# Two fixed experts instead of three, and ScalarE scaling in the low-part route of the expert weights

## The chip, the cores and the metric

One core of a Trainium2 chip runs the whole program. The metric is the device time of one execution in microseconds (us), with the kernel before and the kernel after run on the same chip. TensorE (PE) multiplies matrices, VectorE (DVE), ScalarE (ACT) and GpSimd (POOL) work elementwise, SyncE (SP) issues most DMA transfers.

## The reference

Attention over 4 batches, 12 heads, 448 positions and 64 columns gives 1792 tokens of 768 numbers. A dense two-matrix layer with a leaky ReLU follows. The last layer is a routed one, and it is the part that the change touches:

```python
skip_score = x @ w_skip
do_compute = skip_score > 0
xc = x[do_compute]
logits = xc @ w_gate
e_idx = np.argmax(logits, axis=1)
...
for e in range(E):
    mask = e_idx == e
    h = np.maximum(xc[mask] @ w1[e], 0.0)
    y[mask] = gate_w[mask, None] * (h @ w2[e])
out[do_compute] = xc + y
```

There are E = 8 experts; w1[e] is 768 x 1024 and w2[e] is 1024 x 768. With the inputs of seed 0, 691 tokens are routed, and the reference gives experts 0 to 7 the counts 155, 107, 80, 162, 52, 62, 65 and 8.

## The kernel before

The program has three stages on one timeline: attention, the dense layer in 8 blocks of tokens, and the experts. The experts' stage is a sequence of eight passes, numbered 0 to 7 here. A pass takes the tokens of one expert, in a fixed number of columns (WIDTHS, line 251), because the program is compiled before the counts are known. The first FIXED passes (line 250) belong to the experts of the same number, 176 columns each. The other passes belong to the other experts ranked by their token counts (`ranks`, `ranked`): the largest gets 176 columns, the next 128, 96, 80 and 64. A fixed expert's weights can be fetched at any time; a ranked expert's can be fetched only when the rank is known, with an address read from a register (`load_ids`, line 1718). Tokens beyond a width are treated in a loop behind everything (line 1817), which runs no time when all fit.

A pass e gathers its rows (POOL, line 1460), turns them by transposes (PE, line 1476; ACT line 1480 writes the high half zh, DVE line 1483 the low half zl), multiplies by w1 ("up e", lines 1443 to 1445, into hp; ACT 1498 and DVE 1501 make hh and hl), multiplies by w2 ("down e", the same lines, into yp; ACT 1515), transposes back (PE, line 1524), adds on DVE (line 1530) and scatters (POOL, line 1536). Every product is three float16 products: high by high, high by low, low by high. So every weight matrix is needed as a high and a low float16 part. Up 0, up 1, down 0, up 2, down 1, up 3, down 2, up 4, down 3, up 5, down 4, up 6, down 5, up 7, down 6, down 7 is the order on PE (`uses`, line 1353; LAG = 3).

A matrix comes in pieces, 12 of 128 x 512 for w1 and 8 of 128 x 768 for w2 (`matrix_steps`, from line 1368). SP loads a piece into one of 8 staging buffers (line 1388). The high part is made by ACT (line 1394) or, where the planner finds ACT busy, by DVE with a tensor_scalar (line 1396). The low part is made by DVE in one scalar_tensor_tensor (line 1401), except for every fourth piece (LO_G = 4) of matrices 6 to 15 of the list, where POOL multiplies the staged piece by 16 (line 1404) and then subtracts the high part (line 1408). The finished matrix lies in one of 6 places: two in a pool "we" (list numbers 0, 1, 6, 7, 12, 13), four in a pool "big" (the others), and in each pool a matrix takes over the place of the one that came four (two) tiles ahead of it in that pool. So number 9 of the list waits until PE has finished number 3. GATE = (4, 4) says which piece is the first that waits until POOL has issued the first gathers; all pieces ahead of it are loaded during the dense layer.

The order on every engine is fixed when the program is built: a planner (`Plan`) with a table of costs picks at each moment the step that can begin first. Each engine then works through its queue in that order on the chip. The planner's costs know nothing of one engine slowing another.

Of the kernel before, what the change touches and what calls it, by code (L numbers as in the profile page):

```python
# [14 lines left out]
AF = mybir.ActivationFunctionType  # L15
ALU = mybir.AluOpType
# [9 lines left out]
SC_W = 16.0  # L26
# [5 lines left out]
class Plan:  # L32
# [50 lines left out]
    def op(self, key, opts, after=(), takes=(), uses=(), dma=False):  # L83


        s = Plan.Step()
        s.dma = dma or (isinstance(opts, tuple) and opts[0] == "Y")
        s.key, s.takes, s.uses = key, list(takes), list(takes) + list(uses)
        s.opts = {}
        for e, ns, f, *h in ([opts] if isinstance(opts, tuple) else opts):  # L90
            hold, more = ns if isinstance(ns, tuple) else (ns, 0)
            s.opts[e] = (hold, more, f, h[0] if h else 0)
        s.outs, s.ready, s.done, s.end, s.engine = [], dict.fromkeys(s.opts, 0), False, 0, None
        s.id = self.count
        self.count += 1
        for b in s.uses:
            b.left += 1
        s.left = 0
        for d in after:
            if d is None:  # L100
                continue
            if d.done:
                self.after(s.ready, d)
            else:
                d.outs.append(s)
                s.left += 1
        if s.left == 0:
            self.enter(s)
        return s
# [97 lines left out]
def attention_moe_routed_experts(  # L207
# [18 lines left out]
    V, A, G, T, Y = nc.vector, nc.scalar, nc.gpsimd, nc.tensor, nc.sync  # L226
# [16 lines left out]
    CAP = 128 + cap2  # L243
# [3 lines left out]
    N_X = 4  # L247


    FIXED = 3  # L250
    WIDTHS = [CAP] * FIXED + [CAP, 128, 96, 80, 64]
    NR = NE - FIXED

    const = ctx.enter_context(tc.tile_pool(name="const", bufs=1))
# [10 lines left out]
    sixteen = const.tile([128, 1], F32, name="sixteen")  # L265
# [47 lines left out]
    op, buf = plan.op, plan.buf  # L313
# [40 lines left out]
    def late_constants():  # L354
# [20 lines left out]
        V.memset(mcount, 0.0)  # L375
        for e, width in enumerate(WIDTHS):
            V.memset(widths[:, e:e + 1], float(width))
# [99 lines left out]
    AHEAD1, AHEAD2 = 2500, 8000  # L477
    LAG = 3
    XFER, TAIL2, N_ST3, UP2 = 1150, 3500, 1, 2740
    GATE, LO_G = (4, 4), 4  # L480
    PLACES = ["st2", "st", "st2", "st", "st2", "st", "st2"] + ["st3"] * N_ST3
    K_WIN, K_WOUT, K_ROUTER = 0, 520, 1200
    done_win = {}
# [867 lines left out]


    uses = sorted([(e, x) for e in range(NE) for x in range(2)], key=lambda u: 2 * u[0] + LAG * u[1])
    b_w, n_w, w_ready, gates = {}, [None], {}, [None]

    def matrix_place(i, pool, name):

        u = uses[i]
        b_w[u] = buf(name)
        b_w[u].left += 1  # L1360

        def new():
            got["we", u] = expert_view(pool.tile([128, BIG], F16, tag="big", name="we"), u[1])

        n_w.append(take(40000 + 100 * i, b_w[u], new, after=n_w[-1:]))
        w_ready[u] = []

    def matrix_steps(i, first=0, last=None):

        e, second = u = uses[i]  # L1370
        n_new = n_w[i + 1]
        src_of = (w1, w2)[second]

        def rows(c):
            if e < FIXED:
                return lambda: src_of[e, c * 128:(c + 1) * 128, :]
            return lambda: src_of[ds(got["id", e], 1), c * 128:(c + 1) * 128, :].rearrange("a p f -> (a p) f")

        for x, (src, at, n) in list(enumerate(expert_pieces(second, rows)))[first:last]:
            got["pieces"] = got.get("pieces", -1) + 1  # L1380
            own = PLACES[got["pieces"] % (len(PLACES) if i >= 6 else 7)]
            b_st = buf(own)
            w = {}

            def load(w=w, src=src, n=n, own=own):
                if "st" not in w:
                    w["st"] = (stage if own == "st" else got[own]).tile([128, DM], F32, tag="st", name="ew")[:, 0:n]
                Y.dma_start(out=w["st"], in_=src())

            def hi(eng, w=w, at=at):  # L1390
                def f():
                    o = at(got["we", u], 0)
                    if eng is A:
                        A.activation(o, w["st"], AF.Copy, scale=SC_W)  # L1394
                    else:
                        V.tensor_scalar(o, w["st"], SC_W, None, op0=ALU.mult)
                return f

            def lo(w=w, at=at):
                h, l = (at(got["we", u], a) for a in range(2))  # L1400
                V.scalar_tensor_tensor(l, w["st"], SC_W, h, op0=ALU.mult, op1=ALU.subtract)  # L1401

            def lo_scale(w=w, n=n):
                G.tensor_tensor(w["st"], w["st"], sixteen.to_broadcast([128, n]), op=ALU.mult)

            def lo_rest(w=w, at=at):
                h, l = (at(got["we", u], a) for a in range(2))
                G.tensor_tensor(l, w["st"], h, op=ALU.subtract)

            def gate(w=w, n=n, own=own):  # L1410
                w["st"] = (stage if own == "st" else got[own]).tile([128, DM], F32, tag="st", name="ew")[:, 0:n]
                G.memset(w["st"][:, 0:1], 0.0)

            key = 40000 + 100 * i + x
            small_ = n < DM
            after, takes, w_uses = [n_new], [b_st], []
            if (i, x) == GATE:

                after = gates[0:1] = [op(key, ("G", 100, gate), takes=[b_st], after=[n_new, gates[0]])]
                takes, w_uses = [], [b_st]  # L1420
            elif (i, x) > GATE:
                after = [n_new, gates[0]]
            if e >= FIXED:
                after = after + [n_ids]
            n1 = op(key, ("Y", (450, XFER * n // 768), load), takes=takes, uses=w_uses, after=after)
            n2 = op(
                key - 0.2,
                [("A", 520 if small_ else 733, hi(A)), ("V", 335 if small_ else 469, hi(V), 500)],
                uses=[b_st, b_w[u]], after=[n1],
            )  # L1430
            if x % LO_G == LO_G - 1 and i >= 6:
                n3 = op(key - 0.25, ("G", 1001 if small_ else 1428, lo_scale), uses=[b_st], after=[n2])
                n3 = op(
                    key - 0.3, ("G", 1113 if small_ else 1596, lo_rest), uses=[b_st, b_w[u]], after=[n3]
                )
            else:
                n3 = op(key - 0.3, ("V", 602 if small_ else 869, lo), uses=[b_st, b_w[u]], after=[n2])
            w_ready[u].append(n3)
# [8 lines left out]
    class Pass:  # L1447
# [99 lines left out]
        def fetch(self, e):  # L1547
# [6 lines left out]
                    k0 - 800, ("G", (1040, n), lambda x=x: self.gather(x)), takes=[self.b_rows[x]],  # L1554
                    after=n_kept + [n_slots, n_ranked if e >= FIXED else None], dma=True,
                )
# [197 lines left out]
    with tc.manual_schedule():  # L1754
# [62 lines left out]
        with tc.For_i(0, nw, 1):  # L1817
# [22 lines left out]
            with tc.For_i(0, NE, 1) as e:  # L1840
# [16 lines left out]
                for w, src, at, n in pieces:  # L1857
                    st = stage.tile([128, DM], F32, tag="st", name="ew")[:, 0:n]
# [55 lines left out]
```

## Time and profile before

| what | us |
|---|---|
| median of 3 runs | 994.85 (991.01 to 997.11) |
| the profiled execution | 991.68 |
| its span, first to last instruction | 989.9 |
| PE busy in the span | 819.5 (83%) |
| DVE busy | 694.2 (70%) |
| ACT busy | 572.6 (58%) |
| POOL busy | 362.3 (37%) |

Times in rows are us from the start of the span. Busy shares are means over the three stages, so a stage is read from its own stretch: the experts' products begin at 817.42 and end at 981.87.

### The profile page before, as it was taken

Reading aid. Unit: us, or ns where it says so; the run is one execution under the profiler, and the core shown is the slowest. Engines: PE = TensorE matmul, PEld = TensorE weight load, DVE = VectorE, ACT = ScalarE, POOL = GpSimd, SP = SyncE. Lnnn points to the kernel's source line nnn. Section 1 sums busy time; section 2 is a strip of 40 time slices with the busy share of each in tenths; the row PEclk is TensorE's granted clock in tenths of the full one; section 3 lists DMA queues with packets and bytes.
Section 4 is the critical chain, followed back from the end, with each engine's and each line's share of the span. In section 5 each row is a group of like instructions: output and inputs, shape, how many; then the busy total and the mean of one; then the engine's idle time right before and its main releaser. Section 6 shows DMA issues by size and latency. Waiting matters only on the chain. (4 is left out here: it accounts for less than half of the span.)

```text
span 989.9 us, 22385 instructions
## 1 busy us (share of the span) xinstructions
PE 819.5 (83%) x8325; PEld 597.1 (60%) x8325; DVE 694.2 (70%) x1611; ACT 572.6 (58%) x1298; POOL 362.3 (37%) x567
## 2 busy tenths in 40 slices
PE   2334448985988998999999899999999859999896
PEld 1213226772545565655665577677686628999896
DVE  6978887798658667888888668242323566889982
ACT  5777887788656665556676556121122336666661
POOL 3545574446325134342332001000101131476893
PEclk9955559986989999999999999999999978999999
DMA  6798988989999999779778956110104458877871
GB/s 187 195 192 201 228 205 174 215 211 213 179 218 191 200 196 187 154 157 171 158 146 169 157 126 223 33 32 29 37 1 161 148 165 303 264 246 254 282 259 34
DMA packets 272834, 170.72 MB, mean 172 GB/s; under 512 B 226086, under 2 KB 239526, under 8 KB 272720
## 3 DMA queue, kind: packets, MB, share of 16 engines
q1 hardware_dynamic: 270464, 161.86, 69.0%
q0 software_dynamic: 1536, 5.42, 1.7%
q10 hardware_dynamic: 720, 1.97, 0.7%
q8 instruction: 67, 1.10, 0.5%
q14 instruction: 47, 0.39, 0.1%
HBM read 100.91 MB, written 14.30 MB: 116 GB/s over the span
## 5 line engine op out<-in xcount | busy, mean ns | idle before, releaser
L1028 PE MATMUL hp<-xh,win 128*128 128x256 f16 (+1 forms) x768 | 193.9, 263 | 3.0 <-DVE gf L1047 3.0
L1029 PE MATMUL hp<-xl,win 128*128 128x256 f16 (+1 forms) x768 | 193.3, 262 | 0.0
L1030 PE MATMUL hp<-xh,win 128*128 128x256 f16 (+1 forms) x768 | 193.2, 262 | 0.0
L1116 PE MATMUL zp<-wout,g_h 128*128 128x384 f16 (+1 forms) x448 | 149.6, 334 | 4.6 <-ACT g_h L1054 2.6
L1118 PE MATMUL zp<-wout,g_l 128*128 128x384 f16 (+1 forms) x448 | 149.0, 333 | 0.4 <-DVE g_l L1061 0.4
L1117 PE MATMUL zp<-wout,g_h 128*128 128x384 f16 (+1 forms) x448 | 148.8, 332 | 0.0
L1401 DVE SCALAR_TENSOR_TENSOR we<-ew,we 128x512 f16<-128x512 f32 (+1 forms) x136 | 133.9, 1026 | 13.6 <-ACT we L1394 13.2
L911 DVE SCALAR_TENSOR_TENSOR p<-sp,r,p 128x448 f16<-128x448 f32 x168 | 111.0, 679 | 37.9 <-ACT p L905 37.0
L890 ACT ACTIVATE sp<-sp,m 128x448 f32<-128x448 f32 x168 | 102.0, 609 | 50.1 <-DVE m L884 48.6
L877 PE MATMUL sp<-qkT 64*64 64x448 f16 (+1 forms) x672 | 92.6, 417 | 45.3 <-DVE p L911 21.9
L905 ACT ACTIVATE p<-sp,r 128x448 f16<-128x448 f32 x168 | 103.2, 636 | 44.9 <-DMA pt<-p 19.5
L1394 ACT ACTIVATE we<-ew 128x512 f16<-128x512 f32 (+1 forms) x158 | 106.1, 710 | 25.5 <-DMA ew<-in_moe_w_dram 21.9
L884 DVE TENSOR_REDUCE m<-sp 128x2 f32<-128x896 f32 x96 | 92.7, 968 | 18.8 <-PE sp L877 18.5
L1047 DVE SCALAR_TENSOR_TENSOR gf<-gf,oma,hp 128x256 f32<-128x256 f32 (+1 forms) x128 | 50.5, 441 | 63.6 <-ACT gf L1043 63.5
L1028 PEld LDWEIGHTS <-win 128*128 128x128 f16 x768 | 76.0, 99 | 27.6 <-issue 12.9
L877 PEld LDWEIGHTS <-qkT 64*64 64x64 f16 (+1 forms) x672 | 28.4, 117 | 91.2 <-issue 67.8
L1029 PEld LDWEIGHTS <-win 128*128 128x128 f16 x768 | 76.1, 99 | 9.3
L1030 PEld LDWEIGHTS <-win 128*128 128x128 f16 x768 | 76.1, 99 | 6.9
L1445 PEld LDWEIGHTS <-we 128*128 128x128 f16 x768 | 75.6, 100 | 7.4 <-issue 7.4
L1444 PE MATMUL hp<-zl,we 128*128 128x176 f16 (+4 forms) x384 | 71.6, 228 | 6.8 <-DVE zl L1483 6.7
L1061 POOL TENSOR_TENSOR g_l<-gf,g_h 128x512 f16<-128x512 f32 x24 | 32.7, 1361 | 120.7 <-ACT g_h L1054 114.3
L1443 PEld LDWEIGHTS <-we 128*128 128x128 f16 x768 | 75.6, 100 | 0.7
(225 smaller groups left out, 1860.6 us busy)
## 6 DMA issues: line engine op xcount, KB each, us to landing
ew<-in_moe_w_dram SPq DMA_DIRECT2D x96, 256.0 KB, 4.1
ew<-in_moe_w_dram SPq DMA_DIRECT2D x64, 384.0 KB, 5.4
st<-in_moe_w_out_dram SPq DMA_DIRECT2D x31, 384.0 KB, 4.0
st<-in_moe_w_in_dram SPq DMA_DIRECT2D x28, 384.0 KB, 3.8
qk<-in_k_dram SPq DMA_DIRECT2D x24, 224.0 KB, 3.5
qk<-in_q_dram SPq DMA_DIRECT2D x24, 224.0 KB, 3.3
vf<-in_v_dram SPq DMA_DIRECT2D x24, 224.0 KB, 3.7
zd<-zt SPq DMA_DIRECT2D x14, 384.0 KB, 2.8
```

Of the source, the lines that this page charges most:

```text
L877: T.matmul(out=sp[r, j, 0:S].rearrange("p (j c) -> p j c", j=NJ), lhsT=qT[:, r], rhs=kT[:, :, r], start=(x == 0), stop=(x == last),)
L890: A.activation(e, e, AF.Exp, bias=w["m"][:, x:x + 1], scale=1.0, accum_out=w["s"][:, x, S:S + 1])
L905: A.activation(w["p"][:, x, 0, :], w["s"][:, x, 0:S], AF.Copy, scale=w["r"][:, x:x + 1])
L911: V.scalar_tensor_tensor(p[:, 1, :], w["s"][:, x, 0:S], w["r"][:, x:x + 1], p[:, 0, :], op0=ALU.mult, op1=ALU.subtract)
L1028: T.matmul(out=o, lhsT=win(0, c, m), rhs=xh[:, c, :], start=(c == 0), stop=False)
L1029: T.matmul(out=o, lhsT=win(0, c, m), rhs=xl[:, c, :], start=False, stop=False)
L1030: T.matmul(out=o, lhsT=win(1, c, m), rhs=xh[:, c, :], start=False, stop=(c == KD - 1))
L1116: T.matmul(out=zp, lhsT=gh, rhs=wout(0, kk, ws), start=(kk == 0), stop=False)
L1117: T.matmul(out=zp, lhsT=gh, rhs=wout(1, kk, ws), start=False, stop=False)
L1118: T.matmul(out=zp, lhsT=gl, rhs=wout(0, kk, ws), start=False, stop=(kk == KF - 1))
L1394: A.activation(o, w["st"], AF.Copy, scale=SC_W)
L1401: V.scalar_tensor_tensor(l, w["st"], SC_W, h, op0=ALU.mult, op1=ALU.subtract)
```

## The change

FIXED goes from 3 to 2: passes 0 and 1 keep experts 0 and 1, and six experts are ranked, with widths 176, 128, 96, 80, 64 and 64. A second list `loads` has the matrices of fixed experts first; the weights are fetched, and their places given out, in its order, while PE keeps the order of `uses`. GATE moves to (4, 0), the first piece of matrix 4 of the new list. LO_G goes from 4 to 3, and the multiplication by 16 on the low-part route goes from POOL's tensor_tensor to an ACT activation in place.

```diff
-    FIXED = 3
-    WIDTHS = [CAP] * FIXED + [CAP, 128, 96, 80, 64]
+    FIXED = 2
+    WIDTHS = [CAP] * FIXED + [CAP, 128, 96, 80, 64, 64]
...
-    GATE, LO_G = (4, 4), 4
+    GATE, LO_G = (4, 0), 3
...
     uses = sorted([(e, x) for e in range(NE) for x in range(2)], key=lambda u: 2 * u[0] + LAG * u[1])
+
+    loads = sorted(uses, key=lambda u: u[0] >= FIXED)
...
-        u = uses[i]
+        u = loads[i]
...
-        e, second = u = uses[i]
+        e, second = u = loads[i]
...
-            def lo_scale(w=w, n=n):
-                G.tensor_tensor(w["st"], w["st"], sixteen.to_broadcast([128, n]), op=ALU.mult)
+            def lo_scale(w=w):
+                A.activation(w["st"], w["st"], AF.Copy, scale=SC_W)
...
-                n3 = op(key - 0.25, ("G", 1001 if small_ else 1428, lo_scale), uses=[b_st], after=[n2])
+                n3 = op(key - 0.25, ("A", 620 if small_ else 800, lo_scale), uses=[b_st], after=[n2])
```

The planner sees the new costs and widths, so the queues of the experts' stage come out in another order. Three places of it follow; a number behind a name tells tiles of one name apart.

On DVE, where the low parts of w1 of pass 5 begin; that matrix is tile we_11743 before, and zl_11755 belongs to pass 4, hl_11977 to pass 3:

```order
L1483 SCALAR_TENSOR_TENSOR zl_11755<-zp_11756,zh_11754 128x352
L1483 SCALAR_TENSOR_TENSOR zl_11755<-zp_11834,zh_11754 128x352
L1401 SCALAR_TENSOR_TENSOR we_11743<-ew_11744,we_11743 128x512
L1401 SCALAR_TENSOR_TENSOR we_11743<-ew_11752,we_11743 128x512
L1401 SCALAR_TENSOR_TENSOR we_11743<-ew_11813,we_11743 128x512
L1401 SCALAR_TENSOR_TENSOR we_11743<-ew_11816,we_11743 128x512
L1401 SCALAR_TENSOR_TENSOR we_11743<-ew_11820,we_11743 128x512
L1483 SCALAR_TENSOR_TENSOR zl_11755<-zp_11909,zh_11754 128x352
```

Now (w1 of pass 5 is we_11937, w2 of pass 3 is we_11528, zl_11757 and hl_11942 belong to pass 3):

```order
L1403 SCALAR_TENSOR_TENSOR we_11528<-ew_11697,we_11528 128x768
L1485 SCALAR_TENSOR_TENSOR zl_11757<-zp_11826,zh_11756 128x2x128
L1485 SCALAR_TENSOR_TENSOR zl_11757<-zp_11882,zh_11756 128x2x128
L1532 SCALAR_TENSOR_TENSOR rows_10804<-bp_11989,gate1_155,rows_10804 128x384
L1503 SCALAR_TENSOR_TENSOR hl_11942<-hp2_11943,hh_11941 128x2x128
L1532 SCALAR_TENSOR_TENSOR rows_10804<-bp_12039,gate1_155,rows_10804 128x384
L1503 SCALAR_TENSOR_TENSOR hl_11942<-hp2_11996,hh_11941 128x2x128
L1403 SCALAR_TENSOR_TENSOR we_11937<-ew_11939,we_11937 128x512
L1403 SCALAR_TENSOR_TENSOR we_11937<-ew_11981,we_11937 128x512
```

The matrix used to begin while the turns of the following pass went on, beside down 1; it now begins behind the second hl of up 3.

On POOL, the low parts of w2 of passes 6 (we_12849) and 7 (we_13052) at the end of the stage, before:

```order
L1404 TENSOR_TENSOR ew_13115<-ew_13115,sixteen_75 128x768
L1408 TENSOR_TENSOR we_12849<-ew_13115,we_12849 128x768
L1536 DMA out_0_dram<-rows_11831,sidx1_152 1792x768
L1404 TENSOR_TENSOR ew_13300<-ew_13300,sixteen_75 128x768
L1408 TENSOR_TENSOR we_12849<-ew_13300,we_12849 128x768
L1404 TENSOR_TENSOR ew_13357<-ew_13357,sixteen_75 128x768
L1408 TENSOR_TENSOR we_13052<-ew_13357,we_13052 128x768
```

Now (we_12787 and we_12981):

```order
L1410 TENSOR_TENSOR we_12787<-ew_13488,we_12787 128x768
L1410 TENSOR_TENSOR we_12787<-ew_13560,we_12787 128x768
L1538 DMA out_0_dram<-rows_12231,sidx1_152 1792x768
L1410 TENSOR_TENSOR we_12981<-ew_13664,we_12981 128x768
L1410 TENSOR_TENSOR we_12981<-ew_13766,we_12981 128x768
```

Each pair of POOL instructions has become one; the multiplication by 16 stands in ACT's queue.

On DVE, the last low parts of w2 of pass 7, before (we_13052; zl_13447 belongs to pass 7):

```order
L1401 SCALAR_TENSOR_TENSOR we_13052<-ew_13195,we_13052 128x768
L1401 SCALAR_TENSOR_TENSOR we_13052<-ew_13253,we_13052 128x768
L1483 SCALAR_TENSOR_TENSOR zl_13447<-zp_13508,zh_13446 128x2x64
L1401 SCALAR_TENSOR_TENSOR we_13052<-ew_13397,we_13052 128x768
L1483 SCALAR_TENSOR_TENSOR zl_13447<-zp_13568,zh_13446 128x2x64
```

Now (we_12981; rows_12716 are the rows of pass 6, and their two additions need the whole of down 6):

```order
L1403 SCALAR_TENSOR_TENSOR we_12981<-ew_13615,we_12981 128x768
L1398 TENSOR_SCALAR we_12981<-ew_13716 128x768
L1403 SCALAR_TENSOR_TENSOR we_12981<-ew_13667,we_12981 128x768
L1403 SCALAR_TENSOR_TENSOR we_12981<-ew_13716,we_12981 128x768
L1398 TENSOR_SCALAR we_12981<-ew_13769 128x768
L1403 SCALAR_TENSOR_TENSOR we_12981<-ew_13769,we_12981 128x768
L1532 SCALAR_TENSOR_TENSOR rows_12716<-bp_13941,gate1_155,rows_12716 64x384
L1532 SCALAR_TENSOR_TENSOR rows_12716<-bp_13945,gate1_155,rows_12716 64x384
L1403 SCALAR_TENSOR_TENSOR we_12981<-ew_13775,we_12981 128x768
L1403 SCALAR_TENSOR_TENSOR we_12981<-ew_13779,we_12981 128x768
```

Two high parts of this matrix have come from ACT to DVE, and its last two low parts stand behind the additions of pass 6.

## Rows read from the trace of the kernel before

**Rows 1.** Stretches: length, busy us PE, PEld, DVE, ACT, POOL, then clock, DMA, GB/s.

```profile
880.00:900.00 20.00, 19.95 (x251) 19.38 (x249) 19.79 (x20) 13.33 (x24) 12.92 (x10) 1.00 0.83 263
...
920.00:940.00 20.00, 17.50 (x240) 17.30 (x238) 17.95 (x22) 11.88 (x24) 16.29 (x10) 0.91 0.79 269
...
818.00:975.00 157.00, 149.97 (x2227) 145.32 (x2225) 130.77 (x164) 97.13 (x182) 99.84 (x64) 0.97 0.77 255
903.50:966.90 63.40, 58.53 (x1009) 57.58 (x1007) 57.64 (x70) 40.06 (x79) 54.75 (x34) 0.97 0.77 259
```

**Rows 2.** Groups on PE, 740 to 990: busy, mean ns | idle before, releaser.

```profile
L1444 PE MATMUL hp<-zl,we 128*128 128x96 f16 x48 | 7.8, 225 | 2.5 <-DVE zl L1483 2.5
```

**Rows 3.** Waits of SP's load queue, 740 to 990: total us, times, longest.

```profile
SPq L1388 <- DVE we L1401: 57.9, 47, 9.6
```

**Rows 4.** Groups on DVE, 740 to 990: busy us, mean ns | idle before.

```profile
L1401 DVE SCALAR_TENSOR_TENSOR we<-ew,we 128x768 f16<-128x768 f32 x52 | 60.5, 1196 | 8.0 <-ACT we L1394 7.8
L1401 DVE SCALAR_TENSOR_TENSOR we<-ew,we 128x512 f16<-128x512 f32 x60 | 56.0, 978 | 3.9 <-ACT we L1394 3.8
```

**Rows 5.** DVE in order of time: start, us, instruction.

```profile
805.01 3.55 DVE L1401 SCALAR_TENSOR_TENSOR we<-ew,we 128x768 f16<-128x768 f32 x4
835.09 3.09 DVE L1401 SCALAR_TENSOR_TENSOR we<-ew,we 128x512 f16<-128x512 f32 x5
928.99 3.69 DVE L1396 TENSOR_SCALAR we<-ew 128x512 f16<-128x512 f32 x1
954.43 0.32 DVE L1501 SCALAR_TENSOR_TENSOR hl<-hp,hh 128x160 f16<-128x160 f32 x1
954.66 2.01 DVE L1401 SCALAR_TENSOR_TENSOR we<-ew,we 128x768 f16<-128x768 f32 x1
```

**Rows 6.** POOL in order of time: start, us, instruction.

```profile
929.31 1.66 POOL L1408 TENSOR_TENSOR we<-ew,we 128x768 f16<-128x768 f32 x1
930.91 1.47 POOL L1404 TENSOR_TENSOR ew<-ew,sixteen 128x768 f32<-128x768 f32 x1
955.93 2.24 POOL L1408 TENSOR_TENSOR we<-ew,we 128x768 f16<-128x768 f32 x1
```

**Rows 7.** PE in order of time: start, us, instruction.

```profile
873.07 0.25 PE L1443 MATMUL yp<-hh,we 128*128 128x176 f16 x1
876.72 0.91 PE L1476 MATMUL zp<-ident,rows 128*128 128x128 f32 x4
877.56 0.25 PE L1443 MATMUL yp<-hh,we 128*128 128x176 f16 x1
885.71 0.24 PE L1443 MATMUL hp<-zh,we 128*128 128x176 f16 x1
898.14 0.38 PE L1476 MATMUL zp<-ident,rows 128*128 128x128 f32 x2
898.36 0.24 PE L1443 MATMUL yp<-hh,we 128*128 128x176 f16 x1
915.39 0.50 PE L1524 MATMUL bp<-ident,y 128*128 128x128 f32 x3
917.74 0.49 PE L1524 MATMUL bp<-ident,y 128*48 128x128 f32 x3
977.67 0.19 PE L1443 MATMUL yp<-hh,we 128*128 128x64 f16 x1
981.87 0.49 PE L1524 MATMUL bp<-ident,y 128*64 128x128 f32 x3
```

**Rows 8.** The loads of weight pieces: min, median, max ns, first and last start.

```profile
L1388 SPq DMA_DIRECT2D ew<-in_moe_w_dram x112: 328/333/1523, 818.4 to 964.0; - x112
```

**Rows 9.** Groups of DVE's additions into rows and ACT's high parts, 740 to 990.

```profile
L1530 DVE SCALAR_TENSOR_TENSOR rows<-bp,gate,rows 128x384 f32<-128x384 f32 x10 | 6.1, 612 | 4.3 <-PE bp L1524 4.3
...
L1394 ACT ACTIVATE we<-ew 128x768 f16<-128x768 f32 x64 | 51.9, 837 | 15.6 <-DMA ew<-in_moe_w_dram 12.5 <-PE zp L1118 2.7
```

**Rows 10.** A float32 to float16 copy on DVE elsewhere: min, median, max ns.

```profile
L1056 DVE CAST g_h<-gf x10: 416/426/1391, 184.0 to 704.1; 128x512 f16<-128x512 f32 x10
```

## The prediction, made before the changed kernel ran

> **What bounds the kernel now.** The busy shares of the page mix three stages, so I read the stretch of the experts alone. There PE is busy 149.97 of 157.00 us, DVE 130.77, POOL 99.84, ACT 97.13 [rows 1]. PE looks like the bound, and over most of the stretch it is. But towards the end DVE is full too: 19.79 of 20.00 us from 880 on, 57.64 of 63.40 from 903.5 to 966.9 [rows 1]. The few waits that PE has there end at DVE: up 5 (96 columns) came to a stop for 2.5 us because zl stood behind weight pieces in DVE's queue [rows 2]. The queue of loads waits for DVE as well, 57.9 us in 47 times: a staging buffer comes free when its low part is written [rows 3]. So the experts' stage has two bounds close together: PE's columns, and the rate at which DVE, slowed by POOL, turns pieces into low parts.
>
> That slowing is seen piece by piece. Four pieces of 768 with no subtraction of POOL beside them took 3.55 us, 0.89 each, and five of 512 took 3.09, 0.62 each; a piece of 768 beside POOL's subtraction took 2.01 while that took 2.24 [rows 5, 6]. Over the stage 52 and 60 low parts took 116.5 us [rows 4], where 52 x 0.89 + 60 x 0.62 = 83.5 would do. The 33.0 us of difference fall on 48 POOL instructions (24 pairs): 0.69 us of DVE time for each.
>
> **What the change does, part by part.** *Columns.* One pass of 176 columns becomes one of 64. A group of 48 products of 176 lasts from 873.07 to 876.72, 3.65; 144 of 64 last from 977.67 to 981.87, 4.20 [rows 7]. A pass has 288, so 21.9 becomes 8.4: 13.5 us less. Pass 3 also loses the second half of its transposes: 0.84 per group becomes 0.22, three times [rows 7], 1.9 us. PE has 15.4 us less to do. With seed 0 the ranked counts are 162, 80, 65, 62, 52, 8, which fit 176, 128, 96, 80, 64, 64, so the loop behind stays empty.
>
> *The list of loads.* Number 3 of the list, whose place number 9 takes over, was w1 of pass 2 and is now w2 of pass 1. PE is done with the first at the end of up 2, with the second at the end of down 1. Number 9 is w1 of pass 5 both times. In the order given with the change its first low part now stands behind the second hl of up 3. Up 3 begins at 885.71 - 1.9 = 883.8; two groups of 128 columns with their back transposes take 2 x 2.35 (915.39 to 917.74 [rows 7]); hh and hl add some 0.8. So DVE begins with w1 of pass 5 at about 889.3. Of the pieces behind the gate 52 come first; at the mean rate of before, 145.6 us for 112 loads [rows 8], 1.30 each, they are issued by 886, so nothing earlier is late, and some pieces of pass 5 are staged already. The eight pieces that are no longer loaded ahead of the gate cost nothing for that reason, and the same holds for the gate, which stands behind seven gathers and not eight.
>
> *From there DVE decides*, since seven matrices (68 pieces) are still to be made, while PE, unhindered, needs less time than that. DVE's queue from there to the last low part has, counted in the order: 24 low parts of 768 and 24 of 512, 24 x 0.89 + 24 x 0.62 = 36.3; 14 additions into rows at 0.61 [rows 9], 8.5; 18 hl and 12 zl, which I take like the one of 160 columns at 0.32 [rows 5], 9.6; 16 high parts that the planner gave to DVE (it had 2 in all before, 23 now). A high part is not seen alone in this stage; the nearest row is the copy of 128 x 512, 0.416 at least, 0.426 in the median [rows 10], so 9 x 0.42 + 7 x 0.60 (by the ratio 0.89 to 0.62) = 8.0. That is 62.4. An instruction begins some 0.08 before the end shown of the one ahead (954.43 + 0.32 against 954.66 [rows 5]); for the 60 that are no low parts this takes off 4.8: 57.6. POOL has 20 instructions on the low parts in that time (subtractions alone), at 0.69: 13.8. For the high parts' own waits for POOL I take 0.3 each, 4.8; the ends are 0 (the median copy) and 3.3 (the 3.69 of a high part that began at 928.99 and ended as POOL's 930.91 + 1.47 did [rows 5, 6]), and I lean to the copy because POOL's instructions now stand singly. The sum is 76.2. DVE was busy 99% and 91% in the two rows of its full stretches [rows 1]; at 95% it takes 80.2 us. The last two low parts wait for the additions of pass 6, hence for down 6: 1.5 us more. Down 7 then begins at 889.3 + 80.2 + 1.5 = 971.0, where it began at 977.67 [rows 7].
>
> *ACT* gets 28 multiplications, which I price like its high part of 768, 0.84 us at most [rows 9], 23 us in all, and gives 21 high parts to DVE. Its 97.13 of 157 [rows 1] stay far from full; what could hurt is one such instruction ahead of an hh, 0.84 us, and DVE's backlog hides that. *POOL* loses 24 multiplications (1.47 us for a piece of 768 [rows 6]). That alone ends nothing earlier: its worth is in the 0.69 per instruction, counted above.
>
> **The sum.** Down 7 is 6.7 us earlier, and nothing behind it changes (12.2 us to the end of the span). The profiled execution took 991.68, span 989.9; it would take 985.0. It was 3.2 below the median of the runs shown, so beside that median I say 994.85 - 6.7 = 988.
>
> **The rivals.** *TensorE sets the end.* If DVE keeps up, the 15.4 us of columns come out whole: 994.85 - 15.4 = 979.5, and up to 2.5 less where the wait of up 5 goes too. For it: PE's 149.97 of 157, POOL's shorter route, DVE at 83.5 us for all low parts if POOL left it alone. Against it: the place of w1 of pass 5, which leaves DVE without pieces before 889, and the 16 high parts.
>
> *The high parts on DVE wait for POOL* (slower). Both that DVE had before were hit; if each waits the 3.3 us of the row and not 0.3, the tail grows by 16 x 3.0 / 0.95 = 50 us, to 1038. It decides from small amounts: at 0.40 us more per high part the 6.7 us are gone, at 1.0 us more (16.8 us) the kernel is 1% slower, and at twice that 1022. For it: the row at 928.99, which got in only as two POOL instructions back to back had ended. Against it: ten copies of the same kind with a median of 0.426 and a maximum of 1.391 [rows 10] in stages where POOL works as well. The Trainium skill bears on it: the GPSIMD Engine Reference, section "Key points", says that GpSimd shares its SBUF interfaces with VectorE, in contention with DVE instructions that have two SBUF inputs or run in a 2-port perf mode. The traces agree for the first kind (2.01 against 0.89) and, by the one row, for the second; by that rule the change takes pressure off (28 POOL instructions where there were 48) and puts it on (21 more high parts on DVE).
>
> *The clock.* In the stretch from 920 to 940, with the 2.5 us wait, the granted clock was 0.91 and not 1.00 [rows 1]: some of it ran at the lower of the two levels, 1.2 and not 2.4 GHz. If the longer waits before down 6 and down 7 lead to that for the whole of down 7, its 4.20 us become 8.4: 992. I count this inside the forecast's own range.
>
> *The widths don't fit*, and the loop runs over all eight experts with 160 pieces at 1.30 us: over 200 us more. The counts speak against it.
>
> **How the numbers follow.** The forecast (DVE's tail decides, 988) 0.53, its own range 981 to 996; TensorE's end (979) 0.31; the waiting high parts 0.15; the loop 0.01. About 1%, 10 us, is what a measurement of this kernel tells from no change. Below 984.9 lie the second case and a sixth of the first: 0.40. Above 1004.8 lies most of the third and the loop: 0.13. The rest, 0.47, is within 1%. The range, 973 to 1004, reaches from TensorE's end with its waits gone to the point where the waiting high parts cost 1%.
>
> **What would show it.** Right: DVE without weight pieces shortly before 889 and then full to the end; L1398 (the high parts on DVE) near 0.4 to 0.9 us; some 14 us less slowing on the low parts (28 x 0.69 where there were 33); down 7 near 971, and PE with waits before down 6 and down 7 that end at weights. Wrong: PE without a wait from 817 on (then 979), L1398 with a mean over 1.5 us (then slower), the waits of PE at zl or hh growing because ACT is late, or a first up that no longer begins near 817.

## The result and the profile after

The changed kernel takes 982.55 us (median of 4 runs, 977.27 to 983.59), the kernel before beside it 995.98 (4 runs). The ratio is 0.9865, 95% interval 0.9828 to 0.9901: 13.4 us faster, between 10 and 17. The profiled execution took 983.59, span 981.8; that pair differs by only 8.1 us, since the profile of after reached the last logits 2.2 us later than that of before. Two stretches behind the logits carry the change. From the logits (the start of the last lg on DVE) to the first product of up 0 it is 25.3 us before and 23.1 after. From there to the end of the span, the *stretch* of all that follows, it is 172.5 and 164.4.

Busy time by window after; columns as in [rows 1]:

```profile
818.00:975.00 157.00, 144.42 (x2422) 139.03 (x2419) 128.55 (x190) 104.60 (x202) 69.65 (x42) 0.97 0.79 264
888.00:963.00 75.00, 65.42 (x1349) 63.47 (x1346) 67.77 (x103) 53.89 (x109) 47.43 (x29) 0.97 0.89 294
```

PE has 144.42 us to do where it had 149.97 [rows 1], POOL 69.65 where it had 99.84. From 888 to 963 DVE is the busiest engine. The costliest groups of the weight route, which answer to [rows 4]:

```profile
L1403 DVE SCALAR_TENSOR_TENSOR we<-ew,we 128x768 f16<-128x768 f32 x52 | 56.5, 1107 | 9.1 <-ACT we L1396 8.5 <-POOL we L1410 0.5
L1403 DVE SCALAR_TENSOR_TENSOR we<-ew,we 128x512 f16<-128x512 f32 x56 | 43.4, 807 | 5.4 <-ACT we L1396 5.0
...
L1398 DVE TENSOR_SCALAR we<-ew 128x768 f16<-128x768 f32 x11 | 11.6, 1054 | 1.1 <-DMA ew<-in_moe_w_dram 1.1
...
L1398 DVE TENSOR_SCALAR we<-ew 128x512 f16<-128x512 f32 x12 | 7.3, 615 | 0.0
```

DVE's timeline has the lull and, at the end, the two additions ahead of the last low parts (start, us, instruction, idle time before it and what ended it):

```profile
878.98 0.42 DVE L1485 SCALAR_TENSOR_TENSOR zl<-zp,zh 128x256 f16<-128x256 f32 x1 [0.96 <-ACT zh L1482]
884.41 0.62 DVE L1532 SCALAR_TENSOR_TENSOR rows<-bp,gate,rows 128x384 f32<-128x384 f32 x1 [5.01 <-PE bp L1526]
...
887.63 1.28 DVE L1403 SCALAR_TENSOR_TENSOR we<-ew,we 128x512 f16<-128x512 f32 x2
...
966.35 1.13 DVE L1532 SCALAR_TENSOR_TENSOR rows<-bp,gate,rows 64x384 f32<-64x384 f32 x2 [0.79 <-PE bp L1526]
967.79 2.63 DVE L1403 SCALAR_TENSOR_TENSOR we<-ew,we 128x768 f16<-128x768 f32 x2 [0.31 <-ACT we L1396]
```

And PE's timeline of down 6 and down 7, the rows with a wait ahead of them, which answer to [rows 7]:

```profile
957.49 0.20 PE L1447 MATMUL yp<-hh,we 128*128 128x64 f16 x1 [2.68 <-DVE we L1403]
958.76 0.24 PE L1447 MATMUL yp<-hh,we 128*128 128x64 f16 x1 [0.92 <-DVE we L1403]
...
968.80 0.20 PE L1447 MATMUL yp<-hh,we 128*128 128x64 f16 x1 [1.55 <-POOL we L1410]
969.61 0.20 PE L1447 MATMUL yp<-hh,we 128*128 128x64 f16 x1 [0.55 <-DVE we L1403]
970.48 0.20 PE L1447 MATMUL yp<-hh,we 128*128 128x64 f16 x1 [0.61 <-DVE we L1403]
```

PE now stops in the middle of a matrix, at the product that needs a low part (L1447), for DVE's pieces and for POOL's. After 880 these waits and those for zl sum to 12 us (5.6 and 1.5 in yp, 2.2 and 2.0 in hp, two of 0.4); before, PE waited 5.2 us there, all for zl. Down 7 ends at 974.0 where it ended at 981.87 [rows 7]. Over the whole stretch from up 0 to the end of down 7, before and after (columns as in [rows 1]):

```profile
817.42:982.00 164.58, 157.55 (x2433) 152.68 (x2433) 131.91 (x166) 98.75 (x187) 101.48 (x65) 0.97 0.74 245
```

```profile
817.40:974.20 156.80, 144.26 (x2421) 139.33 (x2421) 128.10 (x189) 104.79 (x202) 69.65 (x42) 0.96 0.79 265
```

PE's busy time fell by 13.3 us, and its idle time rose from 7.0 to 12.5: the columns are most of what was gained, and waits took 5.5 us of it back.

### The profile page after: what moved, and what is told of

It reads as the page before. It is cut to its first block, busy times and chain, and to the rows that moved or that the text cites. A ratio compares the mean times of both kernels' runs of the same rounds, so it can differ in the third digit from the quotient of the medians.

```text
span 981.8 us, 22366 instructions
## 1 busy us (share of the span) xinstructions
PE 806.0 (82%) x8313; PEld 583.5 (59%) x8313; DVE 684.6 (70%) x1626; ACT 576.5 (59%) x1305; POOL 328.2 (33%) x545
## 5 line engine op out<-in xcount | busy, mean ns | idle before, releaser
L1403 DVE SCALAR_TENSOR_TENSOR we<-ew,we 128x512 f16<-128x512 f32 (+1 forms) x132 | 117.3, 919 | 16.3 <-ACT we L1396 15.1
L1396 ACT ACTIVATE we<-ew 128x512 f16<-128x512 f32 (+1 forms) x137 | 93.0, 706 | 24.5 <-DMA ew<-in_moe_w_dram 23.5
L1028 PEld LDWEIGHTS <-win 128*128 128x128 f16 x768 | 75.4, 98 | 28.0 <-issue 13.4
L1447 PEld LDWEIGHTS <-we 128*128 128x128 f16 x768 | 75.7, 100 | 13.0 <-DVE we L1403 6.3
L1445 PEld LDWEIGHTS <-we 128*128 128x128 f16 x768 | 75.7, 100 | 1.3 <-issue 0.5
L1446 PEld LDWEIGHTS <-we 128*128 128x128 f16 x768 | 75.8, 101 | 0.2
L1043 ACT ACTIVATE gf<-hp 128x512 f32<-128x512 f32 x56 | 33.4, 596 | 69.2 <-PE hp L1030 63.6
```

The lines of the kernel that those rows point to most:

```text
L1028: T.matmul(out=o, lhsT=win(0, c, m), rhs=xh[:, c, :], start=(c == 0), stop=False)
```

## The experiments

Twelve kernels in three groups (e1 to e4, e5 to e8, e9 to e12), each group beside runs of the kernel before on the same chip; the last group ran on another chip than the first two. The table puts them side by side; all columns but the last are read from one profile of each kernel. "Start" is when the first high part of number 9 (w1 of pass 5) begins, counted from up 0. "Seven" is the time from there to the last low part of number 15, whoever writes it: the seven matrices 9 to 15, 68 pieces. Both are read by giving the instructions of each engine's timeline, in their order, to the tiles of the program's order (to about half a microsecond).

| kernel | logits to up 0 | stretch | start | seven | ratio to before, 95% |
|---|---|---|---|---|---|
| before | 25.3 | 172.5 | 60.6 | 97.1 | 1 |
| changed | 23.1 | 164.4 | 69.3 | 83.7 | 0.9865 (0.9828 to 0.9901) |
| e1 list and widths, old route | 23.3 | 181.0 | 69.1 | 99.1 | 1.0055 (1.0026 to 1.0083) |
| e2 route alone | 25.0 | 169.1 | 59.8 | 85.0 | 0.9942 (0.9907 to 0.9977) |
| e3 changed, high parts on ACT | 21.3 | 169.1 | 69.4 | 85.8 | 0.9905 (0.9871 to 0.9938) |
| e4 places exchanged, first trial | 31.7 | 154.9 | 61.0 | 82.4 | 0.9892 (0.9852 to 0.9932) |
| e5 changed, no low part on POOL | 23.2 | 157.8 | 69.1 | 76.8 | 0.9850 (0.9809 to 0.9891) |
| e6 changed, 48 columns more | 23.1 | 174.6 | 72.8 | 89.1 | 0.9979 (0.9952 to 1.0007) |
| e7 places exchanged | 28.0 | 151.4 | 57.1 | 81.8 | 0.9826 (0.9787 to 0.9866) |
| e8 as e7, no low part on POOL | 28.5 | 151.0 | 59.2 | 78.2 | 0.9813 (0.9771 to 0.9856) |
| e9 as e7, gate and ids moved | 23.5 | 164.8 | 66.0 | 85.6 | 0.9854 (0.9812 to 0.9896) |
| e10 as e9, no low part on POOL | 23.6 | 150.2 | 59.7 | 78.3 | 0.9727 (0.9689 to 0.9765) |
| e11 before, no low part on POOL | 25.2 | 165.9 | 60.9 | 79.7 | 0.9910 (0.9878 to 0.9943) |
| e12 as e7, old route | 27.9 | 171.1 | 57.6 | 100.7 | 0.9971 (0.9945 to 0.9997) |

Three things are to be seen. *Seven* goes with the route: 97 to 101 us with the old one, 82 to 86 with the new one (89 in e6), 77 to 80 without POOL, whatever the places and the number of fixed experts. *Start* goes by the place of number 9: 57 to 61 where it is the place of w1 of pass 2, 69 where it is that of w2 of pass 1 (66 in e9 and 73 in e6 have causes of their own). And the stretch is start + seven + 11 to 14 us in all but three kernels: in e2 and e11 it is 24 and 25 more (PE's columns for three fixed experts end last there), in the kernel before 14.8, where both come together.

**e1 and e2: each half alone.** e1 is the changed kernel with

```diff
-    GATE, LO_G = (4, 0), 3
+    GATE, LO_G = (4, 0), 4
-                A.activation(w["st"], w["st"], AF.Copy, scale=SC_W)
+                G.tensor_tensor(w["st"], w["st"], sixteen.to_broadcast([128, n]), op=ALU.mult)
```

(and the old cost in the planner); e2 is the kernel before with the new lines.

> The changed kernel with the old route of the low parts: every fourth piece, both instructions on POOL. Two fixed experts, the eight widths and the new list of loads stay. Stretch = from the first product of up 0 to the end of the span (172.5 us in the kernel before, 164.4 in the changed one). Theory A (DVE's weight pieces set the tail, columns and list bring the gain): from the first low part of w1 of pass 5 to the last one DVE has 27 low parts of 512 and 24 of 768 (38.1), 12 additions (7.3), 30 hl and zl (9.6), one high part (0.4), less 3.4 of overlap, plus 34 POOL instructions at 0.69 (23.5): 75.5 / 0.95 = 79.5 us, against 78.7 measured in the changed kernel; stretch 163.5 to 167. Rival B (the route through ScalarE brings the gain): stretch 169 or more, low parts of 768 back at 1.16 us. Theory G (the first gather is slowed by the four low parts that the kernel before has beside it): the first gather takes 1.2 us as in the changed kernel, not 3.4.

> The kernel before with the new route alone: each third piece, its multiplication on ScalarE. Three fixed experts, the old widths and the old list stay. Theory A (TensorE's columns were the bound of the kernel before, and its 5.2 us of waits for zl the only part that DVE held): stretch 168.5 to 171.5, that is 1 to 4 us less than the 172.5 of the kernel before. Rival B (the route brings the gain): stretch 166 or less. Rival C (the 15 high parts on DVE eat what POOL gives back): 172 to 175. Theory G: the first gather is slow again, 3.0 to 3.8 us, since the four low parts of 768 stand beside it; if the list of loads has nothing to do with it, 1.2.

e1 measured 181.0, and is slower than the kernel before: theory A fell, the working of the prediction's tail with it. (The 78.7 us that the expectations of e1 and e5 give for the changed kernel end at the additions of pass 6, 966.35; to the last low part, 970.4, it is 82.8.) e2 measured 169.1, as theory A had it. So 0.55% slower and 0.58% faster make 1.35% faster together. PE's longest waits from 950 on in e1, and POOL's last multiplication and low part:

```profile
957.05 0.20 PE L1445 MATMUL hp<-zh,we 128*128 128x64 f16 x1 [3.10 <-ACT we L1396]
960.25 0.23 PE L1447 MATMUL hp<-zh,we 128*128 128x64 f16 x1 [2.97 <-POOL we L1410]
...
974.03 0.24 PE L1447 MATMUL yp<-hh,we 128*128 128x64 f16 x1 [7.10 <-POOL we L1410]
...
985.15 0.20 PE L1447 MATMUL yp<-hh,we 128*128 128x64 f16 x1 [3.96 <-POOL we L1410]
```

```profile
980.86 1.47 POOL L1406 TENSOR_TENSOR ew<-ew,sixteen 128x768 f32<-128x768 f32 x1 [3.74 <-ACT we L1396]
...
983.45 1.65 POOL L1410 TENSOR_TENSOR we<-ew,we 128x768 f16<-128x768 f32 x1
```

DVE's last low part was written at 970.9, POOL's at 985.1. The low parts on DVE were not slower than before (1168 and 875 ns in the mean, 1196 and 978 in [rows 4]). Over its *seven* DVE was busy 69.83 us of 99.10, so DVE was not what held it:

```profile
886.00:985.10 99.10, 73.83 (x1457) 71.58 (x1454) 69.83 (x98) 56.35 (x113) 71.19 (x45) 0.86 0.68 226
```

It is POOL's queue that came last. The same rows of the kernel before show how near that was:

```profile
971.94 1.47 POOL L1404 TENSOR_TENSOR ew<-ew,sixteen 128x768 f32<-128x768 f32 x1 [0.30 <-ACT we L1394]
973.49 1.64 POOL L1408 TENSOR_TENSOR we<-ew,we 128x768 f16<-128x768 f32 x1
```

The last low part for down 7 is done at 975.1, and down 7 began at 977.67 [rows 7]: 2.5 us to spare, with no PE wait that would have shown it. In the 97 us from 878 on POOL was busy 76.73:

```profile
878.00:975.00 97.00, 91.79 (x1558) 90.23 (x1556) 85.22 (x102) 59.61 (x116) 76.73 (x48) 0.98 0.73 242
```

and it waited 22.9 us between 878 and 983 with pairs and scatters in one queue (9.4 for additions, 8.4 for high parts, 3.5 for hl, 1.6 in small ones). Its busy time alone would not name it, as DVE was busier (85.22); but DVE's last low part was done at 966.9, 8 us ahead of POOL's. The loads show it from the other side. What SP waited for between 818 and 970, before (us, times, longest), and in e1:

```profile
SPq L1388 <- POOL we L1408: 37.9, 17, 4.4
SPq L1388 <- DVE we L1401: 36.6, 40, 4.2
```

```profile
SPq L1390 <- DVE we L1403: 40.8, 43, 5.7
SPq L1390 <- POOL we L1410: 35.9, 14, 6.1
```

In the kernel before about as much of that time ends at POOL as at DVE, as 24 of the 112 pieces give back their staging buffer only with POOL's subtraction.

**e3: high parts.**

```diff
-                [("A", 520 if small_ else 733, hi(A)), ("V", 335 if small_ else 469, hi(V), 500)],
+                ("A", 520 if small_ else 733, hi(A)),
```

> The changed kernel with every high part of the experts' stage on ScalarE, so that DVE has none of the 23. Theory A (DVE sets the rate of the tail): 16 high parts, 12.9 us as measured less 1.3 of overlap, leave DVE's tail, which ends up to 12 us earlier; TensorE has 11.7 us of waits after 880 to give, and ScalarE gets 11 us more in a tail where it was busy 54 of 75, so I expect a stretch of 156 to 161. Rival D (the loads set the rate: 0.91 of the DMA engines' time at 303 GB/s): 163 to 166. Rival E (ScalarE is late with hh and zh and with the high parts): over 166, with PE waiting for hh or zh.

169.1, rival E by its number; PE waited 9.6 us for POOL's low parts, not for hh or zh as E had it. With 23 instructions (18.9 us) fewer on DVE, seven took 85.8 and not less. DVE's busy time alone does not set it: over seven it was 64.89 us of 85.70, where the changed kernel has 75.28 of 83.70. But e3 does not rule out ScalarE, which rival E suspects: its busy time rose from 58.67 to 67.71, and DVE's waits for its high parts from 6.1 to 12.0. The changed kernel, then e3 (columns as in [rows 1]):

```profile
886.70:970.40 83.70, 71.49 (x1458) 68.97 (x1455) 75.28 (x110) 58.67 (x118) 52.02 (x31) 0.96 0.80 266
```

```profile
881.60:967.30 85.70, 71.47 (x1457) 69.01 (x1454) 64.89 (x94) 67.71 (x134) 49.20 (x31) 0.93 0.78 260
```

**e5: no low part on POOL.** LO_G = 99, and the edit of e3.

> The changed kernel without any low part on POOL: DVE makes all of them, ScalarE all high parts, the multiplication on ScalarE goes too. Theory P (POOL's instructions slow DVE by about what they save it, and its queue keeps staging buffers and pieces waiting, as with the list alone): from the first low part of w1 of pass 5 DVE has 36 low parts of 512 at 0.62 and 32 of 768 at 0.89 (50.8), 14 additions (8.5), 29 hl and zl (9.3), less 3.4 of overlap: 65.2 / 0.95 = 69 us where the changed kernel took 78.7; TensorE then sets the end: stretch from up 0 to the end of the span 153 to 160 us against 164.4. Rival Q (what POOL takes over is a gain for DVE in full): 20 more low parts, 14.6 us, at the same slowing of the others: stretch 175 or more. In between (POOL neither helps nor hurts): 163 to 167.

157.8, theory P. Seven fell from 83.7 to 76.8. Against the changed kernel DVE has 28 low parts more, but 23 high parts less, and over seven it was busy 66.61 us where it had been 75.28:

```profile
889.20:966.00 76.80, 70.30 (x1457) 68.02 (x1454) 66.61 (x114) 56.03 (x114) 16.43 (x11) 0.96 0.86 290
```

The cleaner pair is e5 against e3, where the high parts stand alike: DVE makes 28 low parts more, its busy time is 66.61 after 64.89, and seven takes 9.0 us less (85.8 to 76.8). Two things go there together, POOL's subtractions and the multiplications on ScalarE that belong to them; no run takes one without the other. What PE still waits for in e5's seven are DVE's low parts (5.0 us). The time of the whole kernel (979.75 us) does not tell it from the changed kernel; the stretch does, and e10 and e11 repeat it.

**e6: columns back.**

```diff
-    WIDTHS = [CAP] * FIXED + [CAP, 128, 96, 80, 64, 64]
+    WIDTHS = [CAP] * FIXED + [CAP, CAP, 96, 80, 64, 64]
```

> The changed kernel with 176 columns for pass 3 where it has 128: 48 columns more, 6.0 us of products (48/176 of 21.9) and 1.9 of transposes for TensorE, nothing more for the weights. Theory A (from 888 on the supply of weight pieces sets the end, TensorE waits): stretch 163 to 167, the waits of down 6 and down 7 shrink by what the columns add. Rival T (TensorE's columns set the end): 171 to 174, waits unchanged. In between would mean that the later places come free too late.

174.6, rival T and a little beyond: 10.2 us for 7.9 us of PE's work. From up 0 to the end of down 7:

```profile
822.30:989.50 167.20, 156.02 (x2433) 149.94 (x2433) 133.06 (x187) 106.00 (x206) 63.98 (x45) 0.94 0.75 250
```

PE's idle time stayed nearly what it was, 11.2 us after 12.5. Its busy time grew by 11.8 us and not by 7.9, at a mean granted clock of 0.94 after 0.96: what lies beyond rival T is more time at the lower clock. That the waits stayed is what speaks against theory A. The table says how: start came 3.5 later and seven took 5.4 longer. Columns hold back the places, places the pieces, and pieces PE: it is a ring, and I had taken the supply for a line with a rate of its own.

**e4 and e7: the place of number 9.** e4 exchanges numbers 3 and 4 in the list and moves the gate as its expectation says; e7 leaves the list and exchanges only the places:

```diff
     loads = sorted(uses, key=lambda u: u[0] >= FIXED)
+    places = loads[:3] + [loads[4], loads[3]] + loads[5:]
...
-        u = loads[i]
+        u = places[i]
...
-        n_new = n_w[i + 1]
+        n_new = n_w[places.index(u) + 1]
```

> The changed kernel with numbers 3 and 4 of the list exchanged (w1 of the first ranked expert ahead of w2 of expert 1), the gate on number 3, and no gate for the loads of the fixed experts: number 9, w1 of pass 5, again takes the place of w1 of pass 2, which is free at the end of up 2 and not at the end of down 1. Theory A (the place of number 9 leaves DVE without pieces, 6.4 us between 884 and 888): DVE begins with w1 of pass 5 before up 3 and the lull goes; stretch 157.5 to 161.5. Rival D (the rate of the loads or of DVE from 888 on decides and takes up what is gained): 163 to 166. Rival F (number 10, w2 of pass 4, now waits for the later place): the lull only moves, 163 to 168.

> The changed kernel with the list of loads as it is, but the places of numbers 3 and 4 exchanged: number 9, w1 of pass 5, takes the place of w1 of pass 2, free at the end of up 2. The gate stays. Some loads of w2 of expert 1 move behind the last write of zd. Theory A (the place of number 9 makes the lull before 888): DVE begins with w1 of pass 5 before up 3; stretch 153 to 159 us, like the 154.9 of the first trial of that place, and from the last logits to up 0 23 to 28 us (23.1 in the changed kernel, 31.7 in that trial, where 14 loads ran beside the gathers). Rival H (that trial gained its stretch only because loads ran ahead of the gathers): stretch 161 to 166.

154.9 and 151.4 against 164.4: theory A, and from up 0 on PE's waits shrink to 4.2 us in e7 (2.1 for zl, 1.2 for a gather, 0.9 without a cause shown). From up 0 to the end of down 7:

```profile
826.26:970.00 143.74, 139.59 (x2421) 135.74 (x2421) 123.30 (x183) 107.78 (x208) 60.97 (x42) 0.99 0.86 288
```

So of the 13 us, 8.4 are idle time of PE that is gone. The other 4.7 are busy time, with as many products as in the changed kernel (x2421) and a mean granted clock of 0.99 after 0.96: with the waits the time at 1.2 GHz went too. DVE's timeline of e7 has no lull like the one above; w1 of pass 5 begins 57.8 us after up 0, where it began 70.2 after it:

```profile
880.77 2.84 DVE L1404 SCALAR_TENSOR_TENSOR we<-ew,we 128x768 f16<-128x768 f32 x3
883.57 0.42 DVE L1486 SCALAR_TENSOR_TENSOR zl<-zp,zh 128x256 f16<-128x256 f32 x1
884.08 1.29 DVE L1404 SCALAR_TENSOR_TENSOR we<-ew,we 128x512 f16<-128x512 f32 x2
```

Most of it was lost ahead of up 0, 28.0 us in e7 and 31.7 in e4: in SP's order the read of the ids (it waits for DVE's ranks) had slipped ahead of the last writes of zd, which the gathers wait for, and loads ran beside the gathers.

**e8, e10, e11: POOL left out elsewhere.** e8 is e7 with the edits of e5. e9 and e10 are e7 and e8 with

```diff
-    GATE, LO_G = (4, 0), 3
+    GATE, LO_G = (3, 3), 3
-    n_ids = op(29000, ("Y", (1500, 0), load_ids), after=[n_ids])
+    n_ids = op(29000, ("Y", (1500, 0), load_ids), after=[n_ids] + n_kept)
```

(LO_G = 99 in e10). e11 is the kernel before with the edits of e5.

> Places of numbers 3 and 4 exchanged and no low part on POOL, all high parts on ScalarE. If theory P and theory A both hold, DVE's pieces are never late and TensorE's columns set the stretch: its busy time from up 0 on is about 142 us, with 12 us behind the last product group: 150 to 156. If POOL's help counts (rival Q): 165 or more. If ScalarE, which has all high parts, is late: PE waits for hh, zh or we of ScalarE, 157 to 165.

> The exchanged places as in the earlier run, with two things put right ahead of up 0: SP reads the ids of the ranked experts behind the last writes of zd (in that run they stood ahead of them, and the first gather began 17.5 us after the last logits where it had been 14.2), and the last five loads of w2 of expert 1 wait behind the gathers. Theory A (the place was the cause in the stretch, SP's order the cause ahead of it): from the last logits to up 0 23 to 24 us, first gather 14.2 after the logits, stretch 151 to 156; with some 795 us ahead of the logits in all runs so far, 971 to 977 us, ratio to the kernel before 0.976 to 0.982. Rival (the five late loads make up 1 or down 1 wait): stretch 157 to 161.

> The same without any low part on POOL and all high parts on ScalarE. If TensorE's columns set the stretch (151.4 and 151.0 with and without POOL in the runs of the exchanged places): 23 to 24 us ahead of up 0 and a stretch of 150 to 155, no difference to the run with POOL beyond 2 us. Rival Q (POOL's help counts once TensorE has no wait): 156 or more, with PE waiting for DVE's low parts.

> The kernel before without any low part on POOL, all high parts on ScalarE; three fixed experts, old list. Theory P (POOL's two instructions give DVE nothing in sum: 33.0 us of slowing for 24 low parts that are worth 12 x 0.89 + 12 x 0.62 = 18.1): stretch 166 to 171.5 against 172.5, the bound being TensorE's columns. Rival Q (POOL's help counts): 176 or more, with PE waiting for DVE.

e8, e10 and e11 came as expected (151.0, 150.2, 165.9). e9 did not: ahead of up 0 it is right (23.5), but the stretch is 164.8, with a start of 66.0. The five loads behind the gate make numbers 6 to 8 later, and more with POOL's low parts than without (59.7 in e10); why by 8 us is open. Of the 13.4 us between e7 and e9, PE's idle time has 7.2 and its busy time 6.1, again at a lower mean clock (0.95 after 0.99):

```profile
817.80:974.90 157.10, 145.70 (x2421) 141.28 (x2421) 126.94 (x190) 110.35 (x212) 64.17 (x42) 0.95 0.84 278
```

What PE still waits for in e10's passes, gathers aside, and the busy times over its stretch:

```profile
PE hp L1447 <- DVE zl L1486: 0.8, 1, 0.8
PE yp L1447 <- issue: 0.6, 1, 0.6
```

```profile
822.00:972.00 150.00, 141.19 (x2426) 136.67 (x2425) 121.43 (x203) 104.92 (x203) 30.00 (x17) 0.98 0.86 292
```

So the loads were no bound in the changed kernel either: over this stretch they run at 292 GB/s, over that of the changed kernel at 264. e10 takes 970.81 us (median of 6) and beats both kernels: its interval, 0.9689 to 0.9765, lies below that of the change.

**e12: the fourth of a square.** e7 with the lines of e1.

> The exchanged places with the old route: every fourth piece, both instructions on POOL. Two fixed experts, eight widths. It makes the fourth of a square: late place with the old route 181.0 us of stretch, late place with the new route 164.4, early place with the new route 151.4. Theory A (the late place squeezes the last seven matrices, and only there is the route worth its 16.6 us): stretch 151 to 157. Rival R (POOL's pairs are too slow for two fixed experts whatever the place): 163 or more, with down 6 and down 7 waiting for POOL's low parts.

171.1: theory A fell again, rival R holds. PE waited 5.2 us for POOL's low parts in down 6 and down 7, as R had it, and another 8.6 for zl, which R had not. The place is worth 9.9 us with the old route (181.0 to 171.1) and 13.0 with the new one; the route 16.6 and 19.7. With two fixed experts they nearly add up. Only with three is the route worth little (172.5 to 169.1), as PE's columns end there 24 us after the last low part.

## Why the prediction was right, and where it was not

*Columns: right.* "PE has 15.4 us less to do." With the supply out of the way on both sides, e11 against e10, the stretch is 165.9 and 150.2: 15.7. Between the two kernels of the change PE's busy time fell by 13.3.

*The place of number 9: right.* Forecast: DVE without pieces, then w1 of pass 5 at 889.3. It came at 887.63, behind 5.0 and 1.4 us of idle time. e7 took the lull away and 13.0 us with it.

*The terms of DVE's tail: right in size.* The slowing per POOL instruction: 56.5 + 43.4 us of low parts, less 52 x 0.89 + 56 x 0.62 = 81.0, is 18.9, over 28 instructions 0.68; forecast 0.69. High parts: 11.6 + 7.3 = 18.9 us for 23, less 11 x 0.60 + 12 x 0.42 = 11.6, is 0.32 each beyond the copy; forecast 0.3, so the rival in which they wait 3.3 each is gone. The two additions of pass 6 stand ahead of the last two low parts as said. The last low part was done at 970.4, forecast 971.0. PE didn't wait for it ahead of down 7 but inside it, product by product, so down 7 ended at 974.0 and not at 971.0 + 4.2. The 1.2 us, with 0.2 less behind the last group, are why the stretch shrank by 8.1 and not 6.7.

*The cause: wrong in part.* Two sentences failed. The first is "From there DVE decides". In the changed kernel DVE is busy 90% of seven and writes the last low part, but its queue is not a term by itself: e3 took 18.9 us off DVE and the seven matrices took no less time; e5 has 28 low parts more on DVE than e3 and they took 9.0 less; in e1 DVE is busy 70% of them, where the working reckons with 95%. The second is that POOL's lost multiplications end "nothing earlier", that their worth is in the 0.69 each. By that working the old route costs the tail 79.5 us (the expectation of e1) and the new one 80.2. Measured, it is 97 to 101 against 82 to 86. The rows that spoke against it were in the trace: POOL's last low part 2.5 us ahead of down 7, and SP's 37.9 us of waits for POOL beside 36.6 for DVE. I had read SP's waits for DVE alone [rows 3]. So before the change two things ended together, PE's columns and POOL's queue, and each half of the change moved one of them: that is why e1 and e2 give nearly nothing. My sum for the changed kernel came out because there POOL no longer ends last (its last low part is done at 968.7, DVE's at 970.4; from 887 on it is busy 51.67 of 83 us) and DVE, at 74.64, is the busiest engine of a ring that sets the pace. That is luck as far as the change goes: the same working gave e1, the change without its route, 163.5 to 167, and e1 took 181.0.

*"The eight pieces that are no longer loaded ahead of the gate cost nothing": wrong, by a gain of 2.2 us.* The first gather of pass 0, on POOL, before and after:

```profile
806.30 3.39 POOL L1460 DMA_INDIRECT rows<-zd,gidx  x1 [9.96 <-DMA out_dram<-zt]
```

```profile
808.49 1.22 POOL L1462 DMA_INDIRECT rows<-zd,gidx  x1 [9.88 <-DMA out_dram<-zt]
```

Before, four low parts of 768 lie beside it, 805.01 to 808.56 [rows 5]. They are the first four pieces of w2 of expert 1 (number 4 of the old list), which stand behind the twelve of w1 of expert 2. Expert 2 is ranked now, so w2 of expert 1 comes earlier, and its last low part is done at 804.00, ahead of the gather. All three kernels with three fixed experts have 3.39 (before, e2, e11), all others 1.21 to 1.32.

*TensorE sets the end (0.31): not here*, PE waited 12 us after 880. The time alone does not say so: 982.55 lies nearer to this rival's 979.5 than to 988. It is the waits that part the two. With the place exchanged it would have been nearly so.

*The clock.* After PE's waits in down 6 the granted clock fell to 0.50, that is 1.2 GHz, but was back at 1.00 for down 7:

```profile
955.00:960.30 5.30, 1.36 (x22) 1.09 (x23) 5.30 (x9) 4.11 (x5) 5.14 (x2) 0.85 0.99 369
960.30:965.40 5.10, 5.10 (x100) 5.10 (x98) 5.07 (x6) 1.29 (x3) 3.83 (x2) 0.50 0.57 205
966.50:974.50 8.00, 5.29 (x150) 4.78 (x148) 3.61 (x4) 2.82 (x6) 3.10 (x2) 1.00 0.10 22
```

By the busy time of a product in the last two rows (51 and 35 ns) the 100 products at 0.50 took some 1.6 us longer, an estimate. Down 7 did not run at it. From up 0 to the end of down 7 the mean granted clock was 0.99 with 4.2 us of idle time on PE (e7), 0.96 with 12.5 (changed kernel), 0.95 with 11.4 (e9) and 0.94 with 11.2 (e6).

*The sum: the size was off.* Forecast 6.7 us, 988 beside the median of before; measured 982.55. The two stretches of the profiles give 8.1 + 2.2 = 10.3, and 13.4 (10 to 17) were measured. The other 3 us lie within the interval: in the fourteen profiles the last logits begin anywhere between 790.8 and 799.2, in a part of the program that the change hardly touches.

## What to carry to other kernels

An engine that is done 2 us before it is needed shows no wait, and can still be the next bound: look for the end of each supplier's last piece against the start of its use before pricing a change that makes the user faster. Where buffers come free by use, a rate of the supply and a cost of the user are not separate terms; follow the ring, and read the loads' waits for every engine that frees a buffer. And when a helper engine slows the one that it helps, price the whole route: here DVE alone, with 20 of 68 low parts more (17 with the old route) and ScalarE making the high parts, had a stretch shorter by 6.6 us (e5), 6.6 (e11), 14.6 (e10) and 0.4 (e8). The medians of whole kernels show it in e10 and e11; in the other two pairs they don't tell the two apart.

## What the runs showed of the hardware

A gather that POOL issues did not run slower beside DVE's low parts, it stood until they were over. Its 3.39 us end 1.13 us after the last of the four (808.56 to 809.69); in e2 the four lie at

```profile
807.54 3.55 DVE L1401 SCALAR_TENSOR_TENSOR we<-ew,we 128x768 f16<-128x768 f32 x4
```

and the gather runs from 808.85 for 3.39, again 1.15 behind their end; alone it takes 1.22. The Trainium skill, SBUF — State Buffer, section "SBUF: two separate sides", calls what VectorE and GpSimd share an exclusive lock and not a split of bandwidth; these rows agree with that (the low parts read two tiles in SBUF, and the gather reads gidx there). The same shows in scatters: 0.9 us at the least, and 7.5 us at the most in e8 and e11, where DVE makes every low part. Those two end 0.78 and 0.77 us after the last of eight low parts beside them. In e5, where DVE makes every low part too, the longest is 2.3 us: it depends on what lies beside a scatter.

Without any subtraction on POOL the low parts still took 950 and 683 ns in the mean (e5), near the 0.89 and 0.62 that the prediction took for undisturbed ones. So most of the slowing came from POOL's elementwise instructions, but not all: the 0.06 us of difference is there without them, and over 112 and 108 low parts it makes some 7 of the 33.0 us before and some 7 of the 18.9 after. The 0.69 and 0.68 per POOL instruction are too high by that.
